# First-MLP second-layer weights and sums kept in HBM as float32 words and split at use; ten more first-layer parts split anew

## The chip, the cores and the metric

One core of one Trainium2 chip runs the whole kernel. TensorE does the matmuls, VectorE, ScalarE and GpSimd the elementwise work, and SyncE (SP) issues the DMAs. The metric is the device time of one execution in microseconds (us); the granted TensorE clock is 1.00 of full speed in every stage of the profile.

## The reference

A random-feature attention is followed by two MLPs over 4 x 576 = 2304 tokens, with a model width of 512 and a hidden width of 2048, all in float32:

```python
x = phi(q) @ (phi(k).T @ v) / (phi(q) @ sum(phi(k)))        # 4 batches x 8 heads, 128 features
h = x @ moe_w_in;   g = max(h, 0) + alpha * min(h, 0);       x = g @ moe_w_out
h = x @ moe2_w_in;  g = where(h >= 1, h, where(h <= -1, 0, (h + 1)**2 / 4));  out = g @ moe2_w_out
```

## The kernel before

**Splitting.** A float32 matmul is done as three matmuls of a reduced type: each operand is split in a high half (`hi_of`, L269 on ScalarE, L271 on VectorE) and a low half, source minus high half (`lo_of`, L278 and L279 on VectorE, L280 on GpSimd), and `mm3` adds high x high (L285), high x low (L286) and low x high (L287). A pair of halves of a [128, 512] tile has 512 KB, the tile itself 256 KB.

**Stages.** The attention runs over 16 head pairs. As soon as the first batch is done, the first MLP starts on three groups of 512 tokens; its work is interleaved with the rest of the attention. A group has 16 units `f` (slices of 128 hidden columns). In a unit, four hidden products (`h`, first layer, layer index a = 0) of three matmuls each are followed, one unit later, by four output products (`y`, second layer, a = 1). After the three groups come four passes of eight steps that use Winograd's form of the matrix product, seven products of half-size blocks in place of eight: pass 0 is the first MLP for the tokens left over (m = 0), passes 1 to 3 are the second MLP (m = 1). A step `s` needs three sets of first-layer weights: k = 0 (the blocks themselves), k = 1 and k = 2 (sums of blocks, made by `second_parts`; k = 2 holds a plain half block behind the sums). Passes 0 and 1 also take the second layer plainly, from tiles `w_out`.

**Weights.** The inputs come as 64-bit words. `convert` loads one as `raw` (four slots) and turns it into a float32 tile `w` with two operations on ScalarE (L316 or L317 on GpSimd, L319), two on VectorE (L323, L327) and one on GpSimd (L328). First-layer tiles of the first MLP stay in SBUF in the pool `w` until the pool `second` takes their place; the second-layer tiles have five slots that are shared with the second MLP's (`w_slots[1]`), and the second MLP's first-layer tiles have four (`w_slots[0]`). `second_weights` starts the conversion of the second MLP's tile f at unit 12 + 3.4 f (`W2_FROM`, `PACE`).

**Where the halves come from.** `weight_parts` fills the halves `w_parts` that a unit multiplies with; each layer has two slots. A first-layer part is split from the SBUF tile in the first and second group, a second-layer part in the first group only (`split_part`: high half on ScalarE, low half on GpSimd). The last split is stored to HBM as halves (`w_kept`), and the later groups, the sets of pass 0 and its `w_out` tiles load these 512 KB again. The sums of `second_parts` are split at once (`keep`, tile `w_keep`) and stored as halves too.

**The order.** The order of all instructions on all engines is written out when the program is built: `Plan` runs the generators of the code as streams in a model of the engines, and takes at each step the operation that can start first; the rank settles ties, a lower one first (`URGENT` is -10). Each operation has a cost there, as 170 + 2.12 n ns for a two-input operation of n columns on GpSimd, and a DMA has 60 + bytes / 340 ns and another 2800 ns until it counts as landed. An operation may name several engines, of which the one that ends first is taken; "dve2" and "pool" exclude each other in the model, as users of "ports". On the chip each engine works its list off in order, and an instruction whose input is late holds up what stands behind it.

Of the kernel before, what the change touches and what calls it, by code (L numbers as in the profile page):

```python
# [176 lines left out]
def favor_attention_two_mlps(  # L177
# [47 lines left out]
    PACE = 34  # L225
# [106 lines left out]
    w_slots = [Tokens(range(n)) for n in W2S]  # L332
# [79 lines left out]
    def weight_parts(a):  # L412
        for i, (g, f) in enumerate(units):
            t = yield part_slots[a]
            j, u = divmod(f, 2)
            fresh = g < 2 - a
            if fresh:
                yield ev("w", 0, f, a)
            else:
                yield ev("stored", 0, j, place_of(a, u))  # L420
            both = part_tile(t, "w_parts")
            parts[i, a] = both[:, 0, :], both[:, 1, :], t
            if fresh:
# [4 lines left out]
    def split_part(a, i, both, store):  # L428
        g, f = units[i]
        yield from split(both, weights[0, f, a])  # L430
        done("part", i, a)
        if a:
            plan.put(w_slots[1], slot_of[0, f, 1])
        if not store:
            return
        j, u = divmod(f, 2)
        k = place_of(a, u)
        plan.add(store_kept(kept[0, j, k], both, (0, j, k)), NU)
        if k == 5:
            plan.add(store_kept(kept[0, j, 2][:, :, DM:], both[:, :, DM // 2 :], (0, j, 6)), NU)  # L440
# [520 lines left out]
    for m in range(2):  # L961
        for j in range(NJ2):
            for k in range(3 if m else 5):
                n = DM if k != 2 else 3 * DM // 2
                kept[m, j, k] = dram.tile([P, 2, n], F32, tag=f"kept{m}_{j}_{k}", name="w_kept")
    for j in range(NJ2):
        kept[0, j, 5] = dram.tile([P, 2, DM], F32, tag=f"odd{j}", name="w_kept")
# [14 lines left out]
    def open_second():  # L982
# [3 lines left out]
        yield ev("part", 2 * NF - 1, 0)  # L986
# [13 lines left out]
    def second_parts(m, j):  # L1000
# [14 lines left out]
        s2, s3, s1, s4 = sa[:, 0, :], sa[:, 1, :], sb[:, 0, :], sb[:, 1, :]  # L1015
        yield either(h, "tensor_tensor", (s1, a21, a22, ALU.add), off_path())
# [4 lines left out]
        plan.add(keep(kept[m, j, 2][:, :, :DM], sa.rearrange("p a n -> p (a n)"), (m, j, 2)), rank)  # L1021
        yield either(h, "tensor_tensor", (s4, a12, s2, ALU.subtract), off_path())
        done("summed", m, j)
        plan.add(keep(kept[m, j, 1], sb.rearrange("p a n -> p (a n)"), (m, j, 1)), rank)
# [5 lines left out]
        for i in range(2):  # L1030
            yield ev("kept", m, j, 2 - i)
            plan.put(sum_slots[i], 0)

# [18 lines left out]
    def load_set(s, k):  # L1052
# [15 lines left out]
        yield _dma(P * n * 8, lambda: nc.sync.dma_start(both.bitcast(F32), kept[m, j, k]))  # L1068
        w_of[s, k] = both[:, 0, :], both[:, 1, :], t
        done("set", s, k)  # L1070

    def load_out():
        yield ev("g", NU - 1)
        for s in range(PLAIN):
            p, j, m = step(s)
            for u in (1, 0):
# [4 lines left out]
                else:  # L1081
                    yield ev("stored", 0, j, 3 + u)
# [5 lines left out]
                else:  # L1088
                    both = tile_of(t, [P, 2, DM], "w_out")
                    out_of[s, u] = both[:, 0, :], both[:, 1, :], t  # L1090
                    plan.add(load(both.bitcast(F32), kept[0, j, 3 + u], ("out part", s, u)), 0)
# [697 lines left out]
```

## Time and profile before

| | us |
|---|---|
| three runs | 888.48, 891.96, 893.24 |
| median | 891.96 |
| profiled execution | 888.5 |
| its span, first to last instruction | 886.7 |
| TensorE busy in the span | 874.5 (99%) |
| VectorE, ScalarE, GpSimd busy | 681.6, 529.0, 302.1 |
| moved by DMA | 242.42 MB |

The engines appear as PE (TensorE matmul), PEld (its weight loads), DVE (VectorE), ACT (ScalarE), POOL (GpSimd) and SP. An engine is busy from the start to the end of an instruction; matmuls overlap, so two starts that lie closer than one matmul is long are no contradiction. "idle before" is the time an engine stood still ahead of an instruction, with the one that released it. Tiles are named by the program, output<-inputs, and L269 is line 269. From the starts of the matmuls, the first MLP begins at 55 us, its second group at 176 us and its third at 302 us; the Winograd steps run from 387 us, the second MLP's from 511 us.

### The profile page before, as it was taken

To read this page: it belongs to the slowest core of one execution; us is meant where nothing else is said; L and a number is where in the kernel's file an instruction comes from. 1 tells how busy PE (TensorE), PEld (TensorE's weight loads), DVE (VectorE), ACT (ScalarE), POOL (GpSimd) and SP (SyncE) were. 2 spreads that over 40 slices of the span, in tenths; PEclk is the share of its full clock that TensorE was granted. 3 is DMA by queue.
4 is the path that set the end of the run, shared out by engine and by line. 5 is a ranking of instruction groups with operands and counts; after the bars stand their busy time and mean duration, and the time that the engine had idled before them with its cause. 6 is when DMAs were issued, how large, how long until landed. Compare 5 with 4: busy or idle time off the path is not lost.

```text
span 886.7 us, 17834 instructions
## 1 busy us (share of the span) xinstructions
PE 874.5 (99%) x6449; PEld 770.0 (87%) x6449; DVE 681.6 (77%) x1239; ACT 529.0 (60%) x1160; POOL 302.1 (34%) x284
## 2 busy tenths in 40 slices
PE   9999999999999999999999999999999999999998
PEld 7677777777777788889999999989999999999998
DVE  6897666777557835869779997977978997588964
ACT  6887777766666522334344566666657765476653
POOL 1667667676548773201514315321000000000000
PEclk9999999999999999999999999999999999999999
DMA  9867676699996999998999979999787778776773
GB/s 231 231 200 222 204 219 212 213 301 304 323 313 251 322 325 342 349 336 281 323 331 327 316 255 324 324 314 317 263 283 250 268 252 284 258 259 214 230 244 122
DMA packets 98360, 242.42 MB, mean 273 GB/s; under 512 B 28384, under 2 KB 36192, under 8 KB 98272
## 3 DMA queue, kind: packets, MB, share of 16 engines
q1 hardware_dynamic: 98112, 241.22, 81.8%
q8 instruction: 51, 0.84, 0.4%
q14 instruction: 37, 0.30, 0.1%
q10 hardware_dynamic: 160, 0.07, 0.0%
HBM read 177.81 MB, written 63.44 MB: 272 GB/s over the span
## 4 chain that ended last, share of the span: by engine, by line
PE 82%; DVE 4%; POOL 4%; issue 4%; DMA 3%; ACT 2%; SPq 2%; ACTq 0%; POOLq 0%; DVEq 0%
PE y L285 11%; PE y L287 11%; PE y L286 11%; PE h L285 10%; PE h L287 10%; PE h L286 10%; PE a L287 4%; PE a L286 4%; PE a L285 4%; DMA raw<-w 3%; PE a L641 2%; POOL w L328 2%; PE a L504 1%; POOL w_parts L280 1%; SPq L301 1%
## 5 line engine op out<-in xcount | busy, mean ns | idle before, releaser
L328 POOL TENSOR_TENSOR w<-w,raw 128x512 uint32<-128x512 uint32 x64 | 89.3, 1401 | 179.2 <-DVE w L327 177.4
L285 PE MATMUL h<-x_hi,w_set 128*128 128x384 f32 x288 | 97.3, 338 | 1.6 <-ACT e L1226 0.8
L287 PE MATMUL h<-x_hi,w_set 128*128 128x384 f32 x288 | 96.9, 337 | 0.0
L286 PE MATMUL h<-x_lo,w_set 128*128 128x384 f32 x288 | 96.8, 336 | 0.0
L285 PE MATMUL y<-g,w_parts 128*128 128x512 f32 x192 | 78.9, 411 | 0.5 <-ACT kf L482 0.5
L285 PE MATMUL h<-x_hi,w_parts 128*128 128x512 f32 x192 | 78.2, 407 | 0.0
L287 PE MATMUL h<-x_hi,w_parts 128*128 128x512 f32 x192 | 75.4, 393 | 0.8 <-POOL w_parts L280 0.7
L287 PE MATMUL y<-g,w_parts 128*128 128x512 f32 x192 | 75.1, 391 | 0.0
L286 PE MATMUL y<-g,w_parts 128*128 128x512 f32 x192 | 75.0, 390 | 0.0
L286 PE MATMUL h<-x_lo,w_parts 128*128 128x512 f32 x192 | 74.9, 390 | 0.0
L280 POOL TENSOR_TENSOR w_parts<-w,w_parts 128x512 fp32r<-128x512 f32 x48 | 63.7, 1334 | 31.7 <-ACT w_parts L269 30.4
L851 DVE TENSOR_SCALAR t<-h,alpha_sb 128x512 f32<-128x512 f32 x48 | 35.8, 745 | 36.8 <-PE h L287 36.7
L285 PE MATMUL y<-w_out,g 128*128 128x256 f32 (+1 forms) x192 | 61.2, 319 | 0.0
L286 PE MATMUL y<-w_out,g 128*128 128x256 f32 (+1 forms) x192 | 61.0, 318 | 0.0
L287 PE MATMUL y<-w_out,g 128*128 128x256 f32 (+1 forms) x192 | 61.0, 318 | 0.0
L285 PEld LDWEIGHTS h<-x_hi,w_set 128*128 128x128 f32 x288 | 54.1, 188 | 6.2 <-DVE c L1245 1.4
L286 PEld LDWEIGHTS h<-x_lo,w_set 128*128 128x128 f32 x288 | 54.1, 188 | 3.5
L316 ACT ACTIVATE raw<-raw 128x512 f32<-128x512 f32 x55 | 37.5, 682 | 32.0 <-DMA raw<-w 31.9
L269 ACT ACTIVATE g<-gates 128x384 fp32r<-128x384 f32 x72 | 37.6, 525 | 31.8 <-PE y L286 21.6
L280 POOL TENSOR_TENSOR w_keep<-w_sum,w_keep 128x512 fp32r<-128x512 f32 x32 | 42.1, 1322 | 35.7 <-ACT w_keep L269 26.6
L287 PEld LDWEIGHTS h<-x_hi,w_set 128*128 128x128 f32 x288 | 54.1, 188 | 0.0
L279 DVE TENSOR_TENSOR g<-gates,g 128x384 fp32r<-128x384 f32 x72 | 40.2, 562 | 17.0 <-ACT g L269 16.9
(232 smaller groups left out, 2673.8 us busy)
## 6 DMA issues: line engine op xcount, KB each, us to landing
w_out<-w_kept SPq DMA_DIRECT2D x72, 512.0 KB, 4.7
w_set<-w_kept SPq DMA_DIRECT2D x64, 512.0 KB, 5.0
raw<-w SPq DMA_DIRECT2D x48, 512.0 KB, 6.4
w_parts<-w_kept SPq DMA_DIRECT2D x48, 512.0 KB, 5.3
w_set<-w_kept SPq DMA_DIRECT2D x32, 768.0 KB, 5.0
w_kept<-w_keep SPq DMA_DIRECT2D x40, 512.0 KB, 5.6
w_kept<-w_keep SPq DMA_DIRECT2D x72, 256.0 KB, 5.9
w_kept<-w_parts SPq DMA_DIRECT2D x32, 512.0 KB, 4.9
```

The lines of the kernel that those rows point to most:

```text
L269: ops = [_act(n, lambda: nc.scalar.activation(hi, src, AF.Copy))]
L279: "dve2": _dve_two(n, lambda: nc.vector.tensor_tensor(*args), bias),
L280: "pool": _pool(n, lambda: nc.gpsimd.tensor_tensor(*args)),
L285: nc.tensor.matmul(out_, wh, mh, start=first, stop=False, skip_group_check=more)
L286: nc.tensor.matmul(out_, wh, ml, start=False, stop=False, skip_group_check=more)
L287: nc.tensor.matmul(out_, wl, mh, start=False, stop=last, skip_group_check=more)
L301: nc.sync.dma_start(dst[to, :], src[of, :])
L316: _act(n, lambda: nc.scalar.activation(f, f, AF.Copy, scale=2.0**-112), 45),
L328: yield _pool(n, lambda: nc.gpsimd.tensor_tensor(d, d, low, ALU.add))
L504: nc.tensor.matmul(o, x[rows, c], om[rows, :], start=True, stop=True)
L641: nc.tensor.matmul(o[r], weights[i], moving[i], start=True, stop=True)
L851: yield _dve(SM + 57, lambda: nc.vector.tensor_scalar(t, h, 0.0, a, ALU.min, ALU.mult))
```

## The change

Second-layer tiles of the first MLP and, from step pair j = 2 on (`SPLIT_EARLY`), the sums of pass 0 are stored in HBM as they are, 256 KB each. A new stream `load_again` fetches the second-layer words for the second and third group and for pass 0 into two SBUF slots taken from the second MLP's four, and `split_again` splits them into the tile that was loaded as halves before. `load_set` loads a set of sums as words into the low half's place and splits it there (`split_word`); the plain half block of set k = 2 has its own tile in HBM and its own load. First-layer parts of units f below 10 (`FRESH`) in the third group are split from SBUF again, so five odd ones are not stored; the pool `second` opens behind the last of them. `PACE` is 0: all conversions of the second MLP may start at unit 12, as slots allow.

```diff
     W2_FROM = 12
-    PACE = 34
+    FRESH = 10
+    SPLIT_EARLY = 2
+    PACE = 0
     THIRD_NS = 485
...
 
-    w_slots = [Tokens(range(n)) for n in W2S]
+    w_slots = [Tokens([2, 3]), Tokens(range(W2S[1]))]
     weights = {}
...
             j, u = divmod(f, 2)
-            fresh = g < 2 - a
+            fresh = g < 2 - a or not a and f < FRESH
             if fresh:
                 yield ev("w", 0, f, a)
-            else:
+            elif not a:
                 yield ev("stored", 0, j, place_of(a, u))
...
             parts[i, a] = both[:, 0, :], both[:, 1, :], t
-            if fresh:
+            if a and g:
+                plan.add(split_again(both, (g, f), ("part", i, a)), URGENT - 1)
+            elif fresh:
                 plan.add(split_part(a, i, both, g == 1 - a), weight_rank(i) - 0.1)
...
         g, f = units[i]
+        j, u = divmod(f, 2)
+        if a:
+            plan.add(store_kept(kept[0, j, 3 + u], weights[0, f, a], (0, j, 3 + u)), NU)
         yield from split(both, weights[0, f, a])
...
         if a:
+            yield ev("stored", 0, j, 3 + u)
             plan.put(w_slots[1], slot_of[0, f, 1])
-        if not store:
+        if a or not store:
             return
-        j, u = divmod(f, 2)
         k = place_of(a, u)
-        plan.add(store_kept(kept[0, j, k], both, (0, j, k)), NU)
+        if k != 5 or f >= FRESH:
+            plan.add(store_kept(kept[0, j, k], both, (0, j, k)), NU)
         if k == 5:
-            plan.add(store_kept(kept[0, j, 2][:, :, DM:], both[:, :, DM // 2 :], (0, j, 6)), NU)
+            plan.add(store_kept(kept[0, j, 6], both[:, :, DM // 2 :], (0, j, 6)), NU)
+
+    again = {}
+    again_slots = Tokens([0, 1])
+
+    def load_again():
+        for n in range(NF, NU + NF):
+            g, f = divmod(n, NF)
+            if g == len(groups):
+                f += 1 - 2 * (f % 2)
+            j, u = divmod(f, 2)
+            yield ev("stored", 0, j, 3 + u)
+            i = yield again_slots
+            w = prep_p.tile([P, DM], F32, tag=f"w0{i}", name="w_again")
+            again[g, f] = w, i
+            plan.add(load(w, kept[0, j, 3 + u], ("again", g, f)), 0)
+
+    def split_again(both, key, what):
+        yield ev("again", *key)
+        w, i = again.pop(key)
+        hi, lo = both[:, 0, :], both[:, 1, :]
+        yield hi_of(hi, w, 600)
+        yield lo_of(lo, w, hi, ("pool", "dve2"))
+        done(*what)
+        last = key[0] == len(groups) and key[1] >= NF - 2
+        plan.put(w_slots[0] if last else again_slots, i)
 
...
     kept = {}
-    for m in range(2):
-        for j in range(NJ2):
-            for k in range(3 if m else 5):
-                n = DM if k != 2 else 3 * DM // 2
-                kept[m, j, k] = dram.tile([P, 2, n], F32, tag=f"kept{m}_{j}_{k}", name="w_kept")
     for j in range(NJ2):
-        kept[0, j, 5] = dram.tile([P, 2, DM], F32, tag=f"odd{j}", name="w_kept")
+        for k in range(3):
+            n = DM if k != 2 else 3 * DM // 2
+            kept[1, j, k] = dram.tile([P, 2, n], F32, tag=f"kept1_{j}_{k}", name="w_kept")
+        for k in (0, 5, 6):
+            n = DM if k != 6 else DM // 2
+            kept[0, j, k] = dram.tile([P, 2, n], F32, tag=f"kept0_{j}_{k}", name="w_kept")
+        for k in range(1, 5):
+            n = 2 * DM if k < 3 and j < SPLIT_EARLY else DM
+            kept[0, j, k] = dram.tile([P, n], F32, tag=f"kept0_{j}_{k}", name="w_word")
     out_pairs = {
...
             yield ev("summed", 0, j)
-        yield ev("part", 2 * NF - 1, 0)
+        yield ev("part", 2 * NF + FRESH - 1, 0)
         w_stack.close()
...
         s2, s3, s1, s4 = sa[:, 0, :], sa[:, 1, :], sb[:, 0, :], sb[:, 1, :]
+        sa, sb = (t.rearrange("p a n -> p (a n)") for t in (sa, sb))
+        early = not m and j < SPLIT_EARLY
+        kept_as = keep if m or early else store_kept
+        to = lambda k: kept[m, j, k][:, :, :DM] if m else halves_of(kept[0, j, k]) if early else kept[0, j, k]
         yield either(h, "tensor_tensor", (s1, a21, a22, ALU.add), off_path())
...
         yield either(h, "tensor_tensor", (s3, a11, a21, ALU.subtract), off_path())
-        plan.add(keep(kept[m, j, 2][:, :, :DM], sa.rearrange("p a n -> p (a n)"), (m, j, 2)), rank)
+        plan.add(kept_as(to(2), sa, (m, j, 2)), rank)
         yield either(h, "tensor_tensor", (s4, a12, s2, ALU.subtract), off_path())
         done("summed", m, j)
-        plan.add(keep(kept[m, j, 1], sb.rearrange("p a n -> p (a n)"), (m, j, 1)), rank)
+        plan.add(kept_as(to(1), sb, (m, j, 1)), rank)
         if m:
...
         for i in range(2):
-            yield ev("kept", m, j, 2 - i)
+            yield ev("stored" if kept_as is store_kept else "kept", m, j, 2 - i)
             plan.put(sum_slots[i], 0)
+
+    def halves_of(t):
+        return t.rearrange("p (a n) -> p a n", a=2)
 
...
             both = second[0].tile([P, 2, n], F32R, tag=t, name="w_set")
-        yield _dma(P * n * 8, lambda: nc.sync.dma_start(both.bitcast(F32), kept[m, j, k]))
         w_of[s, k] = both[:, 0, :], both[:, 1, :], t
+        if m or k == 0:
+            yield from load(both.bitcast(F32), kept[m, j, k], ("set", s, k))
+            return
+        if k == 2:
+            plan.add(load(both[:, :, DM:].bitcast(F32), kept[m, j, 6], ("set rest", s)), 0)
+        if j < SPLIT_EARLY:
+            yield from load(both[:, :, :DM].bitcast(F32), halves_of(kept[m, j, k]), ("set word", s, k))
+        else:
+            word = both[:, 1, :DM].bitcast(F32)
+            yield from load(word, kept[m, j, k], ("set word", s, k))
+            yield from split_word(both[:, :, :DM], word)
+        if k == 2:
+            yield ev("set rest", s)
         done("set", s, k)
+
+    def split_word(both, src):
+        hi, lo = both[:, 0, :], both[:, 1, :]
+        yield hi_of(hi, src, 600)
+        yield lo_of(lo, src, hi, ("dve2", "pool"))
 
...
                         yield ev("stored", "out", *key)
-                else:
-                    yield ev("stored", 0, j, 3 + u)
                 t = yield g_slots
...
                     out_of[s, u] = both[:, 0, :], both[:, 1, :], t
-                    plan.add(load(both.bitcast(F32), kept[0, j, 3 + u], ("out part", s, u)), 0)
+                    plan.add(split_again(both, (len(groups), 2 * j + u), ("out part", s, u)), URGENT - 1)
 
...
             if k == 2 or s < PLAIN:
-                plan.add(load_set(s, k), 0)
+                plan.add(load_set(s, k), URGENT+3)
     for p in range(1 + NG):
...
     plan.add(open_units(), 0)
+    plan.add(load_again(), 0)
     plan.add(load_out(), 0)
...
     plan.add(second_mlp(), 0, -1)
```

## Rows read from the trace of the kernel before

**Rows 1.** The page: busy time, share of the span, instructions; DMA in all
```profile
PE 874.5 (99%) x6449; PEld 770.0 (87%) x6449; DVE 681.6 (77%) x1239; ACT 529.0 (60%) x1160; POOL 302.1 (34%) x284
...
DMA packets 98360, 242.42 MB, mean 273 GB/s; under 512 B 28384, under 2 KB 36192, under 8 KB 98272
```

**Rows 2.** Order of time on PE: start, length, instruction, idle before and releaser
```profile
161.67 0.39 PE L286 MATMUL h<-x_lo,w_parts 128*128 128x512 f32 x1
162.40 0.50 PE L287 MATMUL h<-x_hi,w_parts 128*128 128x512 f32 x1 [0.34 <-POOL w_parts L280]
...
165.44 1.16 PE L504 MATMUL a<-om,kq 64*128 64x128 f32 x14 [0.74 <-ACT lf L482]
...
330.88 0.39 PE L286 MATMUL h<-x_lo,w_parts 128*128 128x512 f32 x1
331.11 0.39 PE L287 MATMUL h<-x_hi,w_parts 128*128 128x512 f32 x1
```

**Rows 3.** Stages: stretch, length, busy PE, PEld, DVE, ACT, POOL, clock, DMA, GB/s
```profile
0.00:56.00 56.00, 51.36 (x879) 39.45 (x880) 45.71 (x99) 43.31 (x126) 24.65 (x38) 1.00 0.85 230
56.00:312.00 256.00, 254.02 (x2194) 196.64 (x2193) 183.68 (x328) 176.44 (x424) 176.70 (x158) 1.00 0.78 259
312.00:400.00 88.00, 87.23 (x396) 73.20 (x395) 54.87 (x80) 27.07 (x46) 30.52 (x32) 1.00 0.96 338
400.00:490.00 90.00, 90.00 (x515) 83.80 (x514) 75.85 (x138) 39.46 (x75) 30.09 (x24) 1.00 0.92 315
490.00:580.00 90.00, 89.88 (x478) 82.01 (x476) 81.25 (x134) 57.15 (x112) 30.88 (x25) 1.00 0.89 306
...
800.00:886.70 86.70, 82.77 (x634) 82.57 (x632) 62.33 (x125) 47.62 (x99) 0.00 (x0) 1.00 0.64 206
```

**Rows 4.** Waits of PE: who waited for whom, us, times, longest
```profile
PE h L285 <- ACT e L1226: 0.8, 1, 0.8
PE h L285 <- DVE c L1245: 0.8, 1, 0.8
```

**Rows 5.** Waits of PE's weight loads
```profile
PEld h L287 <- POOL w_parts L280: 2.0, 3, 0.8
```

**Rows 6.** DMA in 312:400: queue's share; issues, KB each, median us to landing
```profile
q1 hardware_dynamic: 9350, 29.64, 96.0%
...
w_parts<-w_kept SPq DMA_DIRECT2D x26, 512.0 KB, 5.5
...
w_kept<-w_keep SPq DMA_DIRECT2D x10, 256.0 KB, 5.5
...
raw<-w SPq DMA_DIRECT2D x4, 512.0 KB, 7.0
```

**Rows 7.** Groups by shape, whole span: busy us, mean ns | idle before
```profile
L280 POOL TENSOR_TENSOR w_parts<-w,w_parts 128x512 fp32r<-128x512 f32 x48 | 63.7, 1334 | 31.7 <-ACT w_parts L269 30.4 <-POOL w_sum L996 1.0
...
L269 ACT ACTIVATE w_parts<-w 128x512 fp32r<-128x512 f32 x48 | 30.4, 639 | 11.0 <-PE y L287 4.1 <-PE h L287 3.4 <-issue 1.3
...
L279 DVE TENSOR_TENSOR w_keep<-w,w_keep 128x512 fp32r<-128x512 f32 x12 | 8.7, 730 | 1.4 <-ACT w_keep L269 1.4
```

**Rows 8.** Groups by shape, VectorE in 400:510
```profile
L323 DVE SCALAR_TENSOR_TENSOR raw<-raw 128x512 uint32<-128x512 uint32 x11 | 7.4, 682 | 0.5 <-ACT raw L319 0.5
L995 DVE TENSOR_TENSOR e<-e,e 128x384 f32<-128x384 f32 x7 | 7.3, 1039 | 0.4 <-ACT e L1226 0.4
...
L327 DVE TENSOR_SCALAR w<-raw 128x512 uint32<-128x512 uint32 x10 | 4.1, 416 | 0.0
```

**Rows 9.** Line 995 in 530:700: ns min/median/max, first and last start
```profile
L995 DVE TENSOR_TENSOR e<-e,e x14: 544/550/1669, 537.3 to 695.3; 128x384 f32<-128x384 f32 x14
```

**Rows 10.** Order of time on ScalarE
```profile
163.16 0.66 ACT L316 ACTIVATE raw<-raw 128x512 f32<-128x512 f32 x1 [2.17 <-DMA raw<-w]
```

**Rows 11.** Waits of ScalarE in 400:510
```profile
ACT w_keep L269 <- DMA w_kept<-w_keep: 10.1, 8, 2.0
ACT raw L316 <- DMA raw<-w: 8.0, 5, 2.7
```

## The prediction

> **What bounds the kernel now.** I read the busy times first: TensorE 99%, with VectorE at 77%, ScalarE 60% and GpSimd 34%, and 242 MB moved by DMA [rows 1]. A busy TensorE is no proof, because a 512-column matmul is booked at 0.39 us. So I looked at its order of time next: in the first MLP the matmuls start 0.23 us apart, each before the one ahead of it has ended [rows 2]. Where such a spacing holds, nothing waits; the step of 0.73 us from 161.67 to 162.40 is what a wait looks like, 0.5 us lost, of which the busy column shows only 0.34 [rows 2]. Then the table by stage. TensorE is idle 4.6 us before 56 us, 2.0 us in 56:312, 0.8 us in 312:400, 0.0 in 400:490, 0.1 in 490:580, and 3.9 us behind 800, which is the drain of the last results [rows 3]. Last the list of waits: the single ones that another engine causes after the start are 0.8 us twice at the first matmul of a Winograd step [rows 4], and in the first MLP three stalls of 2.0 us in sum for the low half of a first-layer part from GpSimd [rows 5] and 0.7 us for an exponential of the attention [rows 2]. No wait of a TensorE instruction is put down to a DMA. So the path is the matmuls themselves; of the profiled 888.5 us (span 886.7 and 1.8 around it) there are some 2.0 + 0.7 + 0.8 + 0.8 = 4.3 us that a better supply in the changed stages could return, and the rest of the idle time lies in the start and the drain, which the edits hardly touch.
>
> The Trainium skill's page "Perfetto Trace Analysis", section "Identifying the Most-Contended Engine", holds that matmul busy time is a bad measure and that weight-load time is the better one. By its measure 13% of TensorE would be free, some 115 us (an estimate from the page's rule and rows 1); the start-to-start times of rows 2 do not bear that out.
>
> The profiled execution is the lowest of the three runs, 3.5 us under the median of 891.96. Its trace does not show what the other two lost. The stretch with the least room in it is 312:400, where the DMA queue takes 96% of the engines' time [rows 6].
>
> **The change part by part.**
>
> *Bytes.* A hi/lo pair of 512 x 128 words is 524 KB, a word tile 262 KB. Loads that shrink or go: 32 second-layer parts of the second and third group and 16 of the first Winograd pass, 48 x 0.262 = 12.6 MB; ten first-layer parts, 5.2 MB; twelve sets of sums (k = 1 and 2, j from 2 on), 3.1 MB. Stores: sixteen second-layer parts, 4.2 MB; twelve sums, 3.1 MB; five odd first-layer parts, 2.6 MB. Sum 30.8 of 242.4 MB. At the 338 GB/s of 312:400 that is 91 us of transfer time [rows 3], and its worth on the path is 0, since TensorE waits for no transfer there. Nor do the single loads land much sooner: 5.5 us median for 512 KB and 5.5 for a 256 KB store in the same stretch [rows 6]. Bounds: 0 in the profiled execution, and up to the 3.5 us by which the median lies above it, if it is late transfers in the full stretch that cost the other runs this.
>
> *Splits added.* 48 second-layer splits and ten first-layer ones are new; the twelve sums are only split later (behind the load, not ahead of the store). 58 high halves x 0.639 = 37 us of ScalarE. Ten low halves on GpSimd alone x 1.334 = 13 us; 48 on VectorE at 0.730 = 35 us or on GpSimd at 1.334 = 64 us [rows 7]. What covers them: in 312:400 (the third group) ScalarE is idle 61 us, GpSimd 57, VectorE 33 [rows 3], against 16 + 10 splits, 17 us of ScalarE and 13 + 12 to 21 us of the low halves. In 56:312 the idle times are 80, 79 and 72 us against 16 splits. I cost both at 0. Not covered so well is the first Winograd pass (some 400 to 511): VectorE is idle 14.2 us in 400:490 and 8.8 in 490:580 [rows 3], and 16 + 12 splits come in, 28 x 0.730 = 20.4 us. What must make room is the conversion of the second MLP's weights, whose pace is taken away (PACE 34 to 0): eleven of them stand in 400:510 with 7.4 + 4.1 = 11.5 us of VectorE [rows 8], and only four loads for them are issued in 312:400 [rows 6]. If they go to the idle time of 312:400, the pass is loaded by 20.4 - 11.5 = 9 us more, which fits into the 14.2. If they don't, 20.4 exceeds it. I take +0.5 us, with bounds 0 and +20 (below, second rival).
>
> How the two engines share is seen in one operation. The sum of two 128x384 tiles on VectorE takes 0.550 us in the median and at worst 1.669 behind 530 us [rows 9], and its mean is 1.039 in 400:510, where GpSimd works more beside it [rows 8]. So a low half on GpSimd is not free for VectorE: it can hold one of its operations for some 1.669 - 0.550 = 1.1 us. The Trainium skill's page "SBUF — State Buffer", section "SBUF: two separate sides", says that the two share a port pair as an exclusive lock, and that the loser waits out the whole instruction. By it the 28 low halves of the pass, if all were on GpSimd, could hold VectorE for up to 28 x 1.334 = 37 us; by the worst case of rows 9 it is 28 x 1.1 = 31.
>
> *Pace.* All sixteen tiles may be converted from unit 12 on, as their slots come free, but the first-layer ones have two slots in place of four, and a second-layer slot now comes free only when its word is stored, some 5.5 us later [rows 6]. The stalls of the first MLP lie just there, at 162 and 165 us [rows 2], and the cause is ahead of GpSimd: ScalarE's queue stands 2.17 us for a raw tile that has not landed [rows 10], and the high halves and exponentials behind it come late. More conversions at once there can lengthen this; fewer transfers on SP's queue can shorten it. I take -0.3, with bounds -2.0 (the three stalls go) and +4 (twice as much again).
>
> *Waits added.* In the first Winograd pass the high half of a set word stands in ScalarE's or VectorE's queue behind a load that was issued only when the slot came free. The planner reckons 2.8 us + 262 KB / 340 = 3.6 us for it; a load takes 5.5 [rows 6]. So up to 12 x 1.9 = 23 us of waiting, and behind it stand the copies that free TensorE's two hidden banks. The trace has such waits already, 10.1 us in eight for a stored tile and 8.0 us in five for a raw one, up to 2.7 us each, in the same stretch, and TensorE loses 0.0 in 400:490 [rows 11, 3]. I take +0.3, bounds 0 and +23. The words of the second layer are fetched two units ahead and have that time to land: 0.
>
> *Late pool.* The second pool now opens behind the split of unit 41's first-layer part in place of a load of unit 31's. The sums of first-layer pairs, on which it waited before, end at about the same unit (the last is due at unit 40), so 0; at most it delays the 10 us of input sums ahead of the first Winograd step, which would lengthen the 0.8 us wait there. Bounds 0 and +3.
>
> *Queue.* Eight more loads (the rest of set k = 2 by itself) and fifteen fewer transfers on SP: 0.
>
> Sum: 888.5 + 0.5 + 0.3 - 0.3 = 889.0 us. That is 0.06% over the profiled execution and 0.33% under the median; I expect the runs of the changed kernel to lie nearer to their floor because the full stretch has air.
>
> **The rivals.**
>
> *Supply gets better (885.0).* The stalls of the first MLP, 2.7 us, and one of the two step waits go, 888.5 - 3.5 = 885.0, and the shorter transfers keep every run there. For it: DMA at 96% [rows 6]; conversions leave the crowded Winograd passes. Against: these waits are 4.3 us in all and none names a DMA [rows 4, 5].
>
> *VectorE becomes the bound of the first Winograd pass (899).* Place: 400 to 511 us. It decides once VectorE's load of the pass passes the pass's length, that is when fewer than some 6 of the 11 conversions leave it (20.4 less 14.2 = 6.2 us at 1.1 us each). Then 20.4 - 14.2 = 6 us come out as wait, and if a dozen of the low halves are put on GpSimd, 12 x 1.1 us of held VectorE work, 13 us, in part: 6 to 19 us, so 894 to 907; I take the middle. For it: VectorE at 84 and 90% in 400:580 [rows 3]. Against: GpSimd idles 60 of 90 us in 400:490, and the conversions and their stores have until the later passes.
>
> *Late words stop the queues (896).* A third of the 23 us of waiting comes through to TensorE's banks. For it: the order in each queue is fixed, and in the first MLP one such wait of 2.17 us did reach TensorE, with 0.74 [rows 10, 2]. Against: 18 us of the same waits cost nothing in this pass now [rows 11].
>
> *The change moves the bytes and nothing else:* then 888.5 to 892, which is my forecast's own case.
>
> **How the numbers follow.** This kernel can tell a change from none at about 0.5%, 4.5 us: faster is under 887.5, slower over 896.4, against 891.96. Forecast, TensorE stays the bound: 0.44, its own range 887.5 to 893. Better supply: 0.32, all of it faster. VectorE the bound: 0.16; late words: 0.08; both slower in my count, though the lower third of either would still be within the bound. Faster 0.32, same 0.44, slower 0.24. The range runs from 883, just below the floor 888.5 - 4.3 = 884.2 with some room for another order of the attention's matmuls, to 899, where half of the second rival is left out.
>
> **What would show it.** Right: matmul starts 0.23 us apart in the third group, some 211 MB moved, DMA share in 312:400 well under 0.96, TensorE idle under 1 us in 400:490, more than four raw loads there. The second rival: VectorE at 95% or more in 400:510 with TensorE waits for its corner sums. The third: ScalarE waits for word loads of 2 us, followed by TensorE waits for copies. The pace term is wrong if the stalls behind unit 12 grow past 4 us. The prediction as a whole is wrong if TensorE's matmul starts change their spacing anywhere without a wait.

## The result, and the profile after

The changed kernel takes 896.63 us in the median of 7 runs (895.10 to 898.69), the kernel before beside it 891.57 (7 runs, 888.48 to 893.24): ratio 1.0071, 95% interval 1.0054 to 1.0088. It is slower by 5 us, where 889.0 was predicted; the time lies in the range (883 to 899) and over the bound for slower (896.4). The profiled execution took 895.22 us (span 893.4), 6.7 more than the one before.

The page of the changed kernel, busy time, DMA and the chain of waits [rows 1]:

```profile
PE 878.8 (98%) x6449; PEld 771.2 (86%) x6449; DVE 735.4 (82%) x1309; ACT 555.4 (62%) x1210; POOL 308.2 (35%) x280
...
DMA packets 97609, 211.50 MB, mean 237 GB/s; under 512 B 28272, under 2 KB 38128, under 8 KB 97520
...
PE 77%; DVE 12%; DMA 5%; ACT 3%; issue 2%; POOL 1%; SPq 1%; ACTq 0%; DVEq 0%; POOLq 0%
```

The 30.9 MB went as worked out. VectorE took on 54 us, ScalarE 26, GpSimd 6, and VectorE is now 12% of the chain that ended last, where it was 4% before:

```profile
PE 82%; DVE 4%; POOL 4%; issue 4%; DMA 3%; ACT 2%; SPq 2%; ACTq 0%; POOLq 0%; DVEq 0%
```

The stages (stretch, its length, busy PE, PEld, DVE, ACT, POOL, clock, DMA, GB/s) [rows 3]:

```profile
56.00:312.00 256.00, 251.41 (x2172) 193.85 (x2171) 210.00 (x357) 185.19 (x445) 182.56 (x159) 0.99 0.70 227
...
312.00:400.00 88.00, 86.61 (x381) 70.56 (x380) 76.28 (x104) 38.19 (x65) 49.75 (x47) 1.00 0.75 250
400.00:490.00 90.00, 89.88 (x509) 83.52 (x508) 87.50 (x162) 50.24 (x97) 25.97 (x19) 1.00 0.71 232
490.00:580.00 90.00, 89.64 (x483) 82.23 (x482) 82.13 (x143) 55.65 (x106) 23.36 (x17) 1.00 0.79 270
```

VectorE's busy time grew by 26 us in 56:312, by 21 in 312:400, by 12 in 400:490 and by 1 in 490:580. The DMA share in 312:400 fell from 0.96 to 0.75, and TensorE's idle time there rose from 0.8 to 1.4 us; in 56:312 it rose from 2.0 to 4.6.

Idle time does not count everything, so I measured by work. Time passes from the first matmul of unit 0 to that of unit 16 (group 2), from there to step 16 (pass 2), and on to the last matmul; the table has this for the profiled execution of several kernels (the kernels with names are experiments, below):

| | unit 0 at | unit 0 to 16 | unit 16 to step 16 |
|---|---|---|---|
| before | 55.1 | 121.0 | 460.4 |
| changed | 54.8 | 123.9 | 464.7 |
| b_pace0 | 56.1 | 122.6 | 460.8 |
| b_shortraw | 56.2 | 119.0 | 460.7 |
| b_late55 | 56.9 | 118.7 | 460.4 |
| b_extra | 56.9 | 122.3 | 465.4 |
| b_extrapool | 56.9 | 124.3 | 468.2 |
| a_shortadd | 57.5 | 122.4 | 460.7 |
| a_shortraw | 56.9 | 122.4 | 461.6 |

Behind step 16 both kernels take 246.0 us. The first stretch is little evidence: b_extra and b_extrapool have the order of the kernel before on each engine up to 181 us, and took 122.3 and 124.3 where the profile before has 121.0. So the 2.9 us of the first stretch are within what one execution differs from the next. The other 4.3, from unit 16 to step 16, are what the profiled execution lost behind it; the medians are 5.1 us apart. (The profiled execution of b_extrapool took 901.47 us, the longest of its twelve, where their median is 895.87; its 468.2 is no typical value.)

One of these losses in order of time, VectorE first (start, us, instruction, idle before and releaser):

```profile
171.91 2.00 DVE L273 CAST x_hi<-x 128x512 fp32r<-128x512 f32 x2
173.83 1.28 DVE L281 TENSOR_TENSOR x_lo<-x,x_hi 128x512 fp32r<-128x512 f32 x2
175.04 1.50 DVE L273 CAST x_hi<-x 128x512 fp32r<-128x512 f32 x1
...
181.00 0.48 DVE L712 STREAM_TRANSPOSE den<-a 128x288 f32<-128x288 f32 x1
...
182.57 1.33 DVE L281 TENSOR_TENSOR w_parts<-w_again,w_parts 128x512 fp32r<-128x512 f32 x1 [0.37 <-ACT w_parts L271]
```

ScalarE behind it, then GpSimd beside the casts, then TensorE:

```profile
181.51 0.21 ACT L729 COPY num<-a 128x64 f32<-128x64 f32 x1 [2.47 <-DVE den L712]
181.62 0.40 ACT L620 ACTIVATE kvz<-a 128x128 f32<-128x128 f32 x2
```

```profile
172.33 1.30 POOL L282 TENSOR_TENSOR w_parts<-w,w_parts 128x512 fp32r<-128x512 f32 x1 [0.16 <-ACT w_parts L271]
174.83 1.42 POOL L282 TENSOR_TENSOR w_parts<-w,w_parts 128x512 fp32r<-128x512 f32 x1 [1.20 <-ACT w_parts L271]
```

```profile
182.07 1.16 PE L537 MATMUL a<-om,kq 64*128 64x128 f32 x14 [1.47 <-ACT kvz L620]
183.16 0.52 PE L287 MATMUL h<-x_hi,w_parts 128*128 128x512 f32 x1
183.49 0.61 PE L288 MATMUL h<-x_lo,w_parts 128*128 128x512 f32 x1
183.90 0.63 PE L289 MATMUL h<-x_hi,w_parts 128*128 128x512 f32 x1
...
186.46 0.61 PE L289 MATMUL y<-g,w_parts 128*128 128x512 f32 x1
186.89 0.41 PE L287 MATMUL y<-g,w_parts 128*128 128x512 f32 x1
```

The cast at 175.04 takes 1.50 us beside a GpSimd split of 1.42; the shortest cast of that shape takes 0.42. What VectorE owes ScalarE comes late, ScalarE stands 2.47 us, and TensorE 1.47. Then the matmuls start 0.43 us apart and not 0.23, from 183.49 to 186.89: 3.4 us for eight that take 1.8 otherwise. The granted clock is 0.64 in 184:188, some of it at 1.2 GHz and the rest at 2.4, and the 1.6 us that this costs are no idle time in any column. The first added low half, at 182.57, comes after this stall, so it did not cause it.

This stall and its low clock are 2.1 of the 4.3 us. Unit 16 takes 10.3 us here; four experiments that keep every engine's order and cut something else (a_shortadd, a_shortadd2, a_shortraw, a_shortdve) have the stall too, with 0.9 to 1.1 us, no low clock behind it, and 8.2 to 8.4 us for the unit. The executions that were not profiled point the same way. The mean granted clock of the seven executions of the changed kernel is 0.996 to 1.000, 0.9977 in the mean, and 0.9994 to 0.9997 for the kernel before in the four sets of runs that go with the experiments. As (1 - clock) x time that is 2.0 us against 0.3 to 0.5, so some 1.5 of the 5.1 us, 0.17%, are low clock (an estimate from these numbers). All experiments made from the changed kernel lose only 0.3 to 0.6 us so, also those that leave every low half whole (a_shortraw, a_late45, a_words17): whatever is cut, this part comes back, and it is not shown to belong to what was cut.

Which loss the added work makes is a question for experiments.

Further stalls of TensorE at places that run without one before:

```profile
337.30 0.50 PE L288 MATMUL y<-g,w_parts 128*128 128x512 f32 x1 [0.22 <-DVE g L280]
...
393.62 0.50 PE L288 MATMUL y<-g,w_parts 128*128 128x512 f32 x1 [0.67 <-DVE g L280]
...
398.07 0.44 PE L287 MATMUL h<-x_hi,w_set 128*128 128x384 f32 x1 [0.22 <-DVE g L280]
```

All three wait for a `g` of VectorE. With the added low halves cut (a_shortadd, below) the first is gone, the second is 0.53 us and the third still 0.23, so the third is not theirs. Ahead of the one at 337.30 VectorE worked a word part and two low halves of kept weights beside GpSimd:

```profile
330.61 0.97 DVE L281 TENSOR_TENSOR w_parts<-w_again,w_parts 128x512 fp32r<-128x512 f32 x1
331.51 2.93 DVE L281 TENSOR_TENSOR w_keep<-w,w_keep 128x512 fp32r<-128x512 f32 x2
```

### The profile page after: what moved, and what is told of

Same layout as the page of the kernel before. It is cut to its first block, busy times and chain, and to the rows that moved or that the text cites. A ratio compares the mean times of both kernels' runs of the same rounds, so it can differ in the third digit from the quotient of the medians.

```text
span 893.4 us, 17971 instructions
## 1 busy us (share of the span) xinstructions
PE 878.8 (98%) x6449; PEld 771.2 (86%) x6449; DVE 735.4 (82%) x1309; ACT 555.4 (62%) x1210; POOL 308.2 (35%) x280
## 4 chain that ended last, share of the span: by engine, by line
PE 77%; DVE 12%; DMA 5%; ACT 3%; issue 2%; POOL 1%; SPq 1%; ACTq 0%; DVEq 0%; POOLq 0%
PE y L287 10%; PE y L288 10%; PE y L289 10%; PE h L287 9%; PE h L289 9%; PE h L288 9%; PE a L289 4%; PE a L288 4%; PE a L287 4%; DMA raw<-w 2%; PE a L537 2%; PE a L674 2%; DVE nm L504 1%; DVE raw L325 1%; DVE w_parts L281 1%
## 5 line engine op out<-in xcount | busy, mean ns | idle before, releaser
L330 POOL TENSOR_TENSOR w<-w,raw 128x512 uint32<-128x512 uint32 x64 | 94.0, 1474 | 104.5 <-DVE w L329 91.6
L282 POOL TENSOR_TENSOR w_parts<-w,w_parts 128x512 fp32r<-128x512 f32 x58 | 77.2, 1332 | 28.7 <-ACT w_parts L271 18.0
L325 DVE SCALAR_TENSOR_TENSOR raw<-raw 128x512 uint32<-128x512 uint32 x64 | 56.8, 891 | 2.3 <-ACT raw L321 2.2
L271 ACT ACTIVATE g<-h 128x512 fp32r<-128x512 f32 x48 | 28.8, 600 | 38.1 <-DVE h L885 34.2
```

The costliest lines, as they stand in the source:

```text
L271: ops = [_act(n, lambda: nc.scalar.activation(hi, src, AF.Copy))]
L282: "pool": _pool(n, lambda: nc.gpsimd.tensor_tensor(*args)),
L325: lambda: nc.vector.scalar_tensor_tensor(low, e, 0x80000000, low, ALU.bitwise_and, ALU.bitwise_or),
L330: yield _pool(n, lambda: nc.gpsimd.tensor_tensor(d, d, low, ALU.add))
```

## The experiments

**Theory:** the added low halves cost the time, through VectorE, directly or by GpSimd holding it. **Rivals:** the raw loads that land late (ScalarE's queue stands for them [rows 10, 11]), the pace, the high halves on ScalarE. Names with a_ are made from the changed kernel, with b_ from the one before. Unless said otherwise ratios are to the kernel before, with their 95% intervals; the changed kernel has 1.0071.

**1. Raw loads cut, in both kernels** (a_shortraw, b_shortraw).

```diff
...
+        if len(seen_raws) > 16:
+            q = dst.shape[1] // 4
+            dst, src = dst[:, :q], src[:, :q]
...
```

> The changed kernel with the written order kept; after the first 16 weight loads each raw tile is loaded by a quarter of its columns only (the conversion works on stale columns). Theory R (late raw loads stop ScalarE's queue, and what stands behind it reaches TensorE late): the stalls at 142, 151 and 193 us of its trace go, some 2.6 us and what follows from them, so 892 to 894 us against 896.6, or down to 890 if all of the loss hangs on them. Theory V (VectorE runs late, from the added low halves and from GpSimd holding it): 895.5 to 897, the 1.5 us wait at 182 us stays.

> Control: the kernel before with the written order kept and the same short raw loads. If the stalls at 145 to 171 us there come from late raw loads, as read from its trace, 888.5 to 890 us against 891.6; if not, 891 to 892.

Measured: a_shortraw 892.49 us, 1.0015 (0.9998 to 1.0031); b_shortraw 886.58 us, 0.9954 (0.9938 to 0.9969). Late raw tiles and their traffic cost the changed kernel 0.56% and the one before 0.46%. With short loads in both, the change still costs 1.0015 / 0.9954 = 1.0061. It is a loss that both have, and not the difference (0.17% of what a_shortraw gives back can be the low clock of the first section).

**2. Low halves cut, by engine** (a_shortpool, a_shortdve, and b_shortpool as control). The operation stays in its place, with 64 of 512 columns, and each engine keeps its order: 54 of GpSimd's 58 in a_shortpool, 31 of VectorE's 32 in the second and third group in a_shortdve.

```diff
...
+        part = (lo[:, :64], src[:, :64], hi.bitcast(F32)[:, :64], ALU.subtract) if short else args
+        on = {e: part if e in short else args for e in ("dve2", "pool")}
...
```

> The changed kernel with the written order kept; the low halves of the parts that GpSimd makes are computed for 64 of 512 columns, so GpSimd is busy some 60 us less and holds VectorE less. Theory V by way of the held VectorE: the wait at 182 us with the clock drop behind it (3.6 us) and the one at 337 us go, 891 to 893 us. Theory V by VectorE's own load alone: 895 to 897. Theory R: 895.5 to 897.

> The changed kernel with the written order kept; the low halves of the second-layer parts that VectorE makes in the second and third group are computed for 64 of 512 columns, so VectorE works some 15 us less in 180 to 400 us. Theory V by VectorE's own load: the waits at 182, 337 and 393 us go, 890 to 893 us. Theory V by GpSimd's hold alone: 894 to 896. Theory R: 895.5 to 897.

> Control for a_shortpool: the kernel before with its order kept and the GpSimd low halves of its first-MLP parts cut to 64 columns. If the hold of VectorE by GpSimd cost only the changed kernel, 890 to 891.5 us; if it costs both alike, 886 to 888, and a_shortpool says nothing on the change.

Measured: a_shortpool 890.82 us, 0.9998 (0.9982 to 1.0015); a_shortdve 893.19 us, 1.0019 (0.9998 to 1.0040); b_shortpool 889.74 us, 0.9989 (0.9974 to 1.0005). Short VectorE splits give back 0.5 of the 0.7%. Short GpSimd ones give back all of it, though the change added only ten of the 58 there; in the kernel before, where 44 of 48 are cut, they are worth 0.1%. In the profile of a_shortpool the stall at 182.07 is gone and unit 16 takes 6.8 us; in the order of the changed kernel this points to GpSimd's older splits as what makes it. So GpSimd's splits cost hardly anything in the kernel before, and cost time once VectorE and GpSimd have the added work.

**3. Only what was added** (a_shortadd: the added low halves of the second and third group, ten on GpSimd and 31 of 32 on VectorE; a_shortadd2: their high halves too). The order is kept, and the 16 splits of the first Winograd pass stay whole.

```diff
...
-        yield from split(both, weights[0, f, a])
+        yield from split(both, weights[0, f, a], g == 2)
...
+        short = what[0] == "part" and parts[what[1:]][2] != "extra"
+        yield lo_of(lo, w, hi, ("pool", "dve2"), short=("pool", "dve2") if short else ())
...
```

> The changed kernel with the written order kept; of the splits that the change adds in the first MLP (second-layer parts of the second and third group, first-layer parts of the third) only the low halves are cut to 64 of 512 columns, on whichever engine they are; the older splits stay whole. Theory V (the added low halves, by their own time and by GpSimd's hold): back to the kernel before, 890 to 892 us. If the loss came from the conversions that start at once (pace) or from the changed order alone: 894 to 897.

> As a_shortadd, with the added high halves cut to 64 columns too (mostly ScalarE). Theory V: no further gain, 890 to 892 us. A theory that ScalarE's added 23 us count: 1 to 3 us below a_shortadd. Pace or order alone: 894 to 897.

Measured: a_shortadd 891.92 us, 1.0003 (0.9985 to 1.0021); a_shortadd2 892.08 us, 1.0013 (0.9999 to 1.0028). With the added low halves cut the loss is gone within the interval; beyond the 0.17% of low clock that every experiment gives back, 0.4 to 0.5% are theirs. In the table unit 16 to step 16 is back at 460.7, but of these 3.9 us 2.1 lie in unit 16, at the stall ahead of any added low half; the other 1.8 lie in units 22, 37, 46 and 47. That a_shortraw, with every low half whole, stands at 461.6 has for the most part the same reason. It is the medians that carry this result, and the traces place less than half of it. That the added high halves on ScalarE cost anything is not seen.

**4. The pace alone, in the kernel before** (b_pace0).

```diff
-    PACE = 34
+    PACE = 0
```

> The kernel before with PACE 0 alone (four first-layer slots as before, no words, no new splits). If the conversions that start at once are the cause: 894 to 896 us. Theory V: 890 to 892.5.

Measured: 891.11 us, 1.0002 (0.9987 to 1.0017). The pace costs nothing there; with two slots in place of four it was not run alone.

**5. The second layer's words alone** (a_words17).

```diff
-    FRESH = 10
-    SPLIT_EARLY = 2
-    PACE = 0
+    FRESH = 0
+    SPLIT_EARLY = 8
+    PACE = 17
```

> One part of the change done alone: the second layer's words. FRESH 0 (no further first-layer parts are split anew), SPLIT_EARLY 8 (the sums of all eight steps are kept as pairs and not as words) and PACE 17. Left of the change are 32 second-layer parts and 16 of the first Winograd pass that are kept as words and split at use. Nothing is left out. If VectorE's time for these splits is the cause, most of the loss stays: 894 to 897 us. If the ten anew split first-layer parts on GpSimd or the words of the sums carry it: 891 to 893 us.

Measured: 896.87 us, 1.0048 (1.0026 to 1.0069). Most of the loss comes with the words of the second layer. What is left for the words of sums and the ten anew split parts is 0.2%, which the intervals do not tell from zero and the low clock of the changed kernel is enough for.

**6. VectorE's share added to the kernel before** (b_extra), and the same on GpSimd (b_extrapool). This tests whether the added operations are enough by themselves, with one reservation: the planner knows of them and writes the order anew, the same as before up to 181 us and another one behind it, so it tests the operations together with that order.

```diff
...
+                if a:
+                    plan.add(over_again(both, i), URGENT - 1)
...
+    def over_again(both, i):
+        yield ev("half", i, 1)
+        lo = both[:, 1, :]
+        args = lo, lo.bitcast(F32), lo.bitcast(F32), ALU.max
+        n = lo.free_size()
+        yield [_dve_two(n, lambda: nc.vector.tensor_tensor(*args))]
+        done("part", i, 1)
```

> The kernel before, with nothing of the change but VectorE's share of it: each of the 32 second-layer parts that groups 2 and 3 load as a pair gets one more operation on VectorE, its low half against itself (max), 512 columns, ahead of the matmuls that read it. Output and bytes stay, no words, no more splits on ScalarE or GpSimd, PACE 34. By the theory that VectorE's low halves are what the change costs, these 32 x 0.73 us alone bring most of the 0.7%: 893 to 897 us. By the rival that it takes the change's words, order or traffic too: 890.5 to 892.5 us.

> As the run before, but the 32 added operations are subtractions on GpSimd at 1.33 us, the high half less the low one (so these second-layer low halves are wrong). If it is only VectorE's own time that counts: 890.5 to 892.5 us. If what GpSimd holds of VectorE counts as much, as the 0.7% that the changed kernel got back from shorter GpSimd operations says: 893 to 896 us.

Measured: b_extra 895.68 us, 1.0047 (1.0029 to 1.0064); b_extrapool 895.87 us, 1.0052 (1.0029 to 1.0076). Thirty-two operations and the order written for them, no word, no other bytes, no ScalarE work: two thirds of the loss. That only VectorE's own time counts does not fit, since the same number on GpSimd costs as much; experiment 2, where the order is kept, says the same. The operations (ns min/median/max, first and last start), first in b_extra, then in b_extrapool:

```profile
L435 DVE TENSOR_TENSOR w_parts<-w_parts x32: 650/693/1802, 186.1 to 391.4; 128x512 fp32r<-128x512 f32 x32
```

```profile
L435 POOL TENSOR_TENSOR w_parts<-w_parts x32: 1272/1294/1823, 186.2 to 396.8; 128x512 fp32r<-128x512 f32 x32
```

So 32 x 0.693 = 22 us of VectorE (32.6 as they ran, 13 of them over 1 us) cost some 4 us, and 32 x 1.294 = 41 us of GpSimd the same. One way to TensorE can be read at the start of the third group in b_extra, GpSimd, VectorE, then TensorE:

```profile
303.10 1.35 POOL L280 TENSOR_TENSOR w_keep<-w_sum,w_keep 128x512 fp32r<-128x512 f32 x1 [1.45 <-ACT w_keep L269]
306.42 2.36 POOL L741 TENSOR_TENSOR x<-num,den 128x512 f32<-128x512 f32 x2 [1.98 <-DVE den L730]
```

```profile
303.21 1.78 DVE L435 TENSOR_TENSOR w_parts<-w_parts 128x512 fp32r<-128x512 f32 x1
304.92 0.74 DVE L861 TENSOR_SCALAR t<-h,alpha_sb 128x512 f32<-128x512 f32 x1
305.58 0.76 DVE L730 STREAM_TRANSPOSE den<-inv 128x576 f32<-128x576 f32 x1
306.27 2.33 DVE L279 TENSOR_TENSOR x_lo<-x,x_hi 128x512 fp32r<-128x512 f32 x2
```

```profile
308.66 0.50 PE L286 MATMUL h<-x_lo,w_parts 128*128 128x512 f32 x1 [0.71 <-DVE x_lo L279]
...
309.89 0.49 PE L285 MATMUL y<-g,w_parts 128*128 128x512 f32 x1 [0.50 <-ACT g L269]
310.62 0.50 PE L286 MATMUL y<-g,w_parts 128*128 128x512 f32 x1 [0.23 <-DVE g L278]
```

The added operation starts 0.11 us behind a GpSimd split and takes 1.78 us in place of 0.69. `den`, `x` and the last `x_lo` of the attention, two low halves in 2.33 us beside GpSimd, follow late, and TensorE, which is about to begin the group with just this tile, stands three times, 1.44 us in sum. The clock follows:

```profile
304.00:308.00 4.00, 3.92 (x16) 2.58 (x15) 4.00 (x5) 0.00 (x0) 2.02 (x2) 1.00 0.99 340
308.00:312.00 4.00, 2.61 (x7) 1.63 (x8) 3.66 (x7) 1.34 (x3) 1.25 (x3) 0.88 0.71 172
312.00:316.00 4.00, 4.00 (x14) 3.14 (x14) 2.93 (x6) 3.63 (x7) 1.85 (x2) 0.69 0.56 205
```

From unit 32 to 33 b_extra takes 9.6 us where the kernel before takes 5.4. That one place holds 4.2 of its 5.0 us, and in b_extrapool, with 12.5, it holds 7.1 of 7.8. But it is also a place where the order differs. In the kernel before, the last `x_lo` ahead of the third group, which begins at 302.1, stands earlier in VectorE's queue:

```profile
300.44 0.68 DVE L279 TENSOR_TENSOR x_lo<-x,x_hi 128x512 fp32r<-128x512 f32 x1
```

In b_extra the group begins at 305.2 and two of these low halves start at 306.27. How much of the 4.2 us is the added operation and how much the other order is not shown. In the changed kernel unit 32 takes 6.3 us, with the added low halves cut 6.3 as well, so what these cost does not lie there.

**7. The other way around: splits moved to GpSimd** (a_pool24), and raw loads reckoned later as well (a_pool24_late; as in 8, with 4500).

```diff
-    PACE = 0
+    PACE = 24
...
-        yield lo_of(lo, w, hi, ("pool", "dve2"))
+        yield lo_of(lo, w, hi, ("pool",) if what[0] == "part" else ("pool", "dve2"))
```

> The changed kernel, computing all of it, with two edits: the low halves of the second-layer parts that are split from words may stand on GpSimd only, where the change lets either engine take them, and the planner's PACE is 24 instead of 0. Some 30 subtractions of 0.73 us leave VectorE for GpSimd, at 1.33 us each there. The theory that VectorE's own time is what the added splits cost expects most of the 0.7% back: 891 to 893 us, with VectorE's busy time some 20 us lower. The theory that GpSimd holding VectorE is the larger part expects no gain: 895 to 897 us. The theory that late raw loads are the cause expects 895 to 897 too.

> As the run before (second-layer low halves on GpSimd alone, PACE 24), and the planner reckons 4.5 us instead of 2.8 for the first byte of the raw loads of all but the first tiles, so that it writes the splits that read them later into the queues of ScalarE and GpSimd. Nothing is left out. If both causes add up, the splits on VectorE and the raw loads that land late, 888 to 891 us, below the kernel before. If the planner's reckoning of the loads changes nothing on the chip: the time of the run before, within 1.5 us. If the later splits make the parts late for TensorE: over 896 us.

Measured: a_pool24 894.90 us, 1.0038 (1.0021 to 1.0054); a_pool24_late 892.63 us, 1.0004 (0.9987 to 1.0021). The loss is halved and no more, which lies between what was expected for VectorE's own time and for GpSimd's hold; and since a_late45, which moves no split and only has another order, comes as low (1.0036), the half is not shown to come from the move. With the order of experiment 8 on top, no difference to the kernel before is left; 888 to 891 us was expected if both causes add up, and that was missed.

**8. Raw loads reckoned as late as they land** (b_late45, b_late55, a_late45). All of the work is done; only the written order changes.

```diff
...
-    LATENCY = {"pe": 210.0, "pe rows": 210.0, "pe cols": 210.0, "dma": 2800.0}
+    LATENCY = {"pe": 210.0, "pe rows": 210.0, "pe cols": 210.0, "dma": 2800.0, "dma raw": 5500.0}
...
```

The line is that of b_late55; the other two have 4500.

> The kernel before, with one edit: the planner reckons 5.5 us instead of 2.8 for the first byte of the raw loads of all but the first tiles. Nothing is left out. With these loads cut to a quarter the kernel before ran 4.4 us faster. If it is the standing of ScalarE's queue behind raw tiles that cost those 4.4 us, the splits stand later in the queues and part of it comes back: 887.5 to 890 us. If it was the traffic itself, or if the later splits are late for TensorE: 890.5 to 892.5 us.

> The kernel before, with the planner's first byte of these raw loads at 4.5 us instead of 2.8; with 5.5 it ran 886.9 us. If the gain grows as the reckoning nears what a load takes in the profile (5.5 to 7 us): 888 to 890 us. If the 4.8 us were a lucky order of that one kernel: 890.5 to 893 us.

> The changed kernel, with one edit: the planner reckons 4.5 us instead of 2.8 for the first byte of the raw loads of all but the first tiles. Nothing is left out. In the kernel before 5.5 us brought 4.8 us of time; with the low halves on GpSimd the changed kernel gained 2.3. If the order behind late raw tiles and the fuller VectorE are two independent losses: 891.5 to 893.5 us. If a fuller VectorE leaves no room to write the splits later: 895 to 898 us.

Measured: b_late45 889.52 us, 0.9979 (0.9958 to 0.9999); b_late55 886.90 us, 0.9948 (0.9928 to 0.9967); a_late45 894.57 us, 1.0036 (1.0019 to 1.0054), which is 0.35% under the changed kernel and between the two times expected. b_late55 beats both kernels and gets all that cutting the loads got (0.9954), with all of the traffic: another order is enough. ScalarE's waits for raw tiles in 60:312 (us in total, times, longest), before, then b_late55:

```profile
ACT raw L316 <- DMA raw<-w: 16.4, 17, 3.1
```

```profile
ACT raw L317 <- DMA raw<-w: 0.9, 1, 0.9
```

The gain lies where these waits lie: unit 0 to 16 takes 118.7 us, against 121.0, 122.3 and 124.3 in three executions of the order before; the rest is unchanged at 460.4. It is not the whole account: b_late45 has nearly as few of these waits (1.7 us in two) and 118.2 us in that stretch, and its runs, 887.32 to 892.66, gain 0.2% only.

## Why the prediction was wrong

**The step that failed** is the cover of the added splits: "in 312:400 ... ScalarE is idle 61 us, GpSimd 57, VectorE 33 ... In 56:312 the idle times are 80, 79 and 72 us ... I cost both at 0" [rows 3]. The idle time was there and did not cover. The term was +0.5 us for all splits; cutting the first MLP's added low halves alone gives back 0.6 to 0.7% (experiment 3), some 5 to 6 us, of which some 1.5 are low clock that any cut gives back, and 32 operations put in, with the order written for them, cost 4 us. What I compared was a sum of idle time in 88 and 256 us. As far as single traces show, what decides is how late one `x_lo`, `g` or `den` comes when one more operation stands ahead of it in the same queue, and whether it is one of the few for which TensorE has nothing else ready. Such places are the change of group in b_extra (308.66), and in the changed kernel the `g` at 337.30 and the one at the change of stage (393.62).

**GpSimd's hold on VectorE** was measured in the working, 1.1 us for a single worst case [rows 9], and used for the first Winograd pass alone. It counts in the first MLP: 1.78 for 0.69 us there, and 1.50 for 0.42. The rule of the Trainium skill's page "SBUF — State Buffer", section "SBUF: two separate sides", that the loser of the shared port waits out the other's instruction, agrees with this: the added operation ends at 304.99, 0.54 us behind the GpSimd split that ends at 304.45, so most of its own 0.69 us were done only then. That an operation on GpSimd is about as dear as one on VectorE here is what experiment 6 measured, each with its own order.

**The second rival** had the engine right and the place wrong. VectorE did reach 97% in 400:490, but the step 0 to step 8 part of the pass takes 124.3 us against 123.6, and the time was lost ahead of it. Its point of decision, that VectorE's load passes the pass's length, was wrong as well: 76.28 of 88 us in 312:400 was enough. (Its time was added up wrongly too: the middle of 894 to 907 is 900.5, not 899.)

**Clock.** I counted stalls at their length. The one of 1.47 us (182.07) and the three of 1.44 us in sum (308.66 to 310.62 in b_extra) are each followed by 3.4 us at the lower of the two clocks, 1.2 GHz for 2.4, some 1.6 us lost, so they cost twice what the waits show. The length of a stall does not decide this: in a_shortadd2 none follows a stall of 1.43 us, and in a_shortdve none follows 2.56 us (the stall, then the row by stretch with the clock of 1.00):

```profile
195.84 0.66 PE L648 MATMUL a<-ident,qf 128*128 128x128 f32 x4 [2.56 <-ACT qf L523]
```

```profile
196.00:200.00 4.00, 4.00 (x23) 3.37 (x23) 1.02 (x2) 4.00 (x9) 2.82 (x3) 1.00 0.58 206
```

What does decide is open. The stages of [rows 3] have a clock of 1.00 throughout and did not show this price. A spacing that changes without a wait was named as what would make the whole prediction wrong; it was seen, but it is the second half of a stall, not a bound of its own.

**What held.** The bytes: 0, and even cutting raw loads was worth only what the order is worth. The pace: 0 in the kernel before (predicted -0.3). ScalarE's part of the splits: 0 within the interval. Late words: the waits for `w_kept` in 400:510 [rows 11] are gone from the list, and the only wait for a word there is 0.2 us. The words of the second layer were put at 0; ScalarE waits 2.9 us for them in 312:400, in two waits of up to 1.6, and no wait of TensorE names them. The late pool: nothing of size after 580, and of the two waits of [rows 4] one is left, with 0.4 us. "Supply gets better" named a real loss, about 4 us of late raw tiles, but the change did not reach it: ScalarE's waits for them in 60:312 are 14.4 us in thirteen, before 16.4 in seventeen. I had taken its worth as the stalls that name it, 2.7 us.

**Open.** The cuts of experiment 3, with the order kept, show that the added low halves make most of the loss, not at which stall each bit arises: one profile of each kernel is too few for that, as the stretch from unit 0 to 16 in the table shows. Why the changed kernel's executions ran at a lower mean clock is open as well: the stall at 182.07 comes ahead of any added low half. Nor do the interventions add up exactly: GpSimd short (-0.73%), VectorE short (-0.5%) and raw loads short (-0.56%) are three ways to give the same queues air, and sum to more than the loss, even if the 0.17% of low clock is taken from each.

## What to carry to other kernels

Where TensorE is at 98 to 99%, idle time of the other engines is no cover by the sum. An added elementwise operation is not free: here it cost a tenth to a fifth of its own time (4 us for 22 us on VectorE or 41 on GpSimd, the new order included). Look first at what stands ahead of the first tile of a stage. VectorE and GpSimd are to be booked together. And before bytes are saved, ask how early the order expects a load: writing in the 5.5 us that the profile shows, in place of 2.8, gained 0.52% in the kernel before, where this change lost 0.71%.

## What the runs showed of the hardware

A VectorE cast of 128x512 took 0.42 us at the least and 1.50 beside GpSimd; a subtraction 0.65 and 1.80. After stalls of 1.47 us (182.07) and of 1.44 us in three (308.66 to 310.62) the granted clock was 0.50 for 3.4 us and TensorE's matmuls of 512 columns started 0.43 us apart, then 0.23 again; after stalls of 0.67 us (393.62), 1.43 (a_shortadd2) and 2.56 (a_shortdve) no such stretch followed.
